# The forward transform's tail on VectorE, and the memory's denominators spread over partitions by transfers

## The chip, the core and the metric

The kernel runs on one core of a Trainium2 chip. A core has five engines that run side by side, each with its own instruction queue: TensorE (PE, with PEld for its weight loads), VectorE (DVE), ScalarE (ACT), GpSimd (POOL) and SyncE (SP), which here only issues transfers. GpSimd can issue transfers too; they go through a queue of their own (q0 in the profile, "software_dynamic"). The metric is the device time of one execution in microseconds; the times given are of several runs.

## What is computed

Two independent parts whose outputs lie side by side.

Part B multiplies a two-dimensional real spectrum by a complex filter and transforms back (x is 2048 x 576):

```
X = rfft2(x);  y = irfft2(X * (w_r + 1j*w_i), (S, D))
```

Part A is attention with 32 heads of 18 over four segments of 512, with a running memory M and its normalizer z:

```
for s in range(4):
    qs, ks, vs = q[:,:,s], k[:,:,s], v[:,:,s]
    a_dot = softmax(qs @ ks.T * scale + causal) @ vs
    pq = phi(qs);  a_mem = (pq @ M) / (pq @ z + 1e-6)
    o = g * a_mem + (1 - g) * a_dot
    M += phi(ks).T @ vs;  z += sum(phi(ks))
out = concat(o) @ wo
```

Here phi(t) is t + 1 where t > 0 and exp(t) elsewhere, and g is sigmoid(beta), one number a head.

## The kernel before

The order of instructions on every engine is the order in which the program emits them: Python generators are advanced by hand, step by step, and each step emits a few instructions. Products in full precision are made from two halves: a value is rounded to a high part (the type F32R) and the rest is its low part; high by high, high by low and low by high are then added on TensorE.

**Forward transform** (`forward`, to about 73 us). It goes over 16 units u. For each, `prep` takes the sum and the difference of two halves of the input (L125, VectorE, into eo, laid out [128, 2, 3, 128]), rounds eo to the high part h (L126/L127, ACT), and makes the low part l. The input has 289 columns: two full blocks of 128 and a third block with a tail. The low part of the two full blocks is one subtraction on VectorE (L131, 128x512). The third block carries the tail's high part and low part in different rows of the same tile: rows 64 to 96 of h are overwritten in place by their own rest, on GpSimd (L132, 33x256). `f1` then makes 14 matmuls (L142) with the tables tab and tab2, the last of each seven from the third block; `ev0` and `ev1` (L146 ACT, L149 VectorE) move the result out of PSUM, `c1` makes 12 more matmuls (L162). Between these, `load_w` splits the weights of part A: a cast on ACT (L405) and a subtraction on VectorE (L407), and for the last, half-empty block a second subtraction that makes zeros (L408). Pieces of the next stage (butterflies, L205) are taken from a paced queue. The tables are loaded on GpSimd's queue (L167 to L170), the units' input on SP's (L114).

**Projections and the inverse transform** follow (to about 356 us); the change touches them only by the second weight's last block and by the place of a small mask, bm.

**Attention** (`attention`, from about 356 us). A loop of 133 steps t. Each step emits score maxima for a later head (`s1`: matmuls L653 and L666, maxima on VectorE L667 and L661, three PSUM buffers), scores and exponentials of the current head (`s2`: L702 to L712, exponentials on ACT, and in every fourth step four causal selections on GpSimd, L716) and a product with the values (`pv`, L731). Background work is a list `bg` of generators, of which `run_bg(1.2)` advances 1.2 pieces a step. A second list, `lane`, is advanced once a step. What must come a step or two later is put off by `later`.

For the segments g = 1, 2, 3 the background is `mixed(g)`: it interleaves `combine(g-1)`, which finishes the previous segment's output, with `mem1(g,t)` for five tiles t in the order ORD = (4,0,1,2,3), then `oproj(g-1)`, the output projection (L874), in half-groups of seven matmuls. The memory's denominators come from `den` (L785), and `recip` turns them into reciprocals: load as 128x128, add 1e-6, reciprocal (L757), scale by the gate (L759), then split into three bf16 parts (L760 to L763, ACT and GpSimd), stored and loaded again as rc["rd"] with 96 rows. `mem1` then works like this:

```
nc.tensor.matmul(pn[:r],s.Mst[g][:r,t,:r],...)          # L804
(vector or scalar copy)(am[:r],pn[:r])                   # L806
yield
nc.tensor.matmul(pb[:r],s.sel[:,t,:r],s.rc["rd"],...)    # L810: sel spreads 7 heads over 126 rows
nc.vector.tensor_tensor(am[:r],am[:r],pb[:r],op=OP.mult) # L811
yield
```

pn and pb share one PSUM buffer ("post"; the score buffers from step 117 on). In `combine`, `high` (L836) and `low` (L841) split the result for the projection; the low part is on GpSimd before step 117 and on VectorE from then on, and so is the sum L857.

**The tail**, after the loop, finishes segment 3: U is copied (L737), its row sums go to memory (rD, L742) and come back, `recip` runs for them, `last_tile` (L883 to L886, L890) makes the last tiles and `last_proj` (L903) projects them, while what is left of `oproj(2)` runs.

Of the kernel before, what the change touches and what calls it, by code (L numbers as in the profile page):

```python
# [5 lines left out]
F32=mybir.dt.float32; F32R=mybir.dt.float32r  # L6
# [96 lines left out]
class FFT:  # L103
# [4 lines left out]
    def forward(s,xp,cp,pp,wl,xs,consts):  # L108
# [10 lines left out]
        def prep(u,halves=False):  # L119

            x=xin.pop(u)
            eo=xp.tile([128,2,3,128],F32,name="eo",bufs=2)
            h=xp.tile([128,2,3,128],F32R,name="eh",bufs=3)
            for r,op in enumerate((OP.add,OP.subtract)):
                v.tensor_tensor(eo[:,r],x[:,0],x[:,1],op=op)  # L125
                if halves: nc.scalar.copy(h[:,r],eo[:,r])  # L126
            if not halves: nc.scalar.copy(h,eo)  # L127
            yield
            l=xp.tile([128,2,2,128],F32R,name="el",bufs=3)
            for w in (slice(0,1),slice(1,2)) if halves else (slice(0,2),):  # L130
                v.tensor_tensor(l[:,w],eo[:,w,:2],h[:,w,:2].bitcast(F32),op=OP.subtract)  # L131
                nc.gpsimd.tensor_tensor(h[64:97,w,2],eo[64:97,w,2],h[64:97,w,2].bitcast(F32),op=OP.subtract)  # L132
            eh[u],el[u]=h,l
            yield
        def f1(u):
            p=pp.tile([128,2,512],F32,name="f1",tag="f1")
            h,l=eh.pop(u),el.pop(u)
            for r in range(2):
                L=[(h[:,r,0],tab[:,0,r,0]),(h[:,r,1],tab[:,0,r,1]),(h[:,r,0],tab[:,1,r,0]),(h[:,r,1],tab[:,1,r,1]),
                   (l[:,r,0],tab[:,0,r,0]),(l[:,r,1],tab[:,0,r,1]),(h[:99,r,2],tab2[:99,r])]  # L140
                for n,(x,t) in enumerate(L):
                    nc.tensor.matmul(p[:,r,:FP],x,t,start=n==0,stop=n==6)  # L142
            F[u]=p
# [22 lines left out]
        tab2=cp.tile([128,2,FP],F32R,name="ftab2",bufs=1)  # L166
# [173 lines left out]
        flush()  # L340
BF=mybir.dt.bfloat16
ORD=(4,0,1,2,3)
H=32; DH=18; SC=float(DH)**-0.5
NEG=-1.0e30

# [39 lines left out]
class ATT:  # L385
    def __init__(s,nc,tc,io,cp,dp):
        s.nc,s.tc,s.io=nc,tc,io
        s.ident=cp.tile([128,128],F32,name="ident"); s.bm=cp.tile([126,7,19],F32,name="bm")
        s.tri=cp.tile([128,128],BF,name="tri"); s.idb=cp.tile([128,128],BF,name="idb")
        s.Mst=[None]+[cp.tile([126,5,126],F32,name=f"Mst{i}") for i in range(1,4)]  # L390
        s.zst=[None]+[cp.tile([126,5,32],F32,name=f"zst{i}") for i in range(1,4)]
        d=lambda n,sh,dt: dp.tile(sh,dt,name=n)
        s.qkD=[d(f"qkD{i}",[8,3,128,512],BF) for i in range(4)]
        s.reD=[d(f"reD{i}",[24,32,512],BF) for i in range(4)]
        s.pqD=[None]+[d(f"pqD{i}",[576,512],F32) for i in range(1,4)]
        s.vD=[d(f"vD{i}",[4,128,622],F32) for i in range(4)]
        s.dp=dp
    def consts(s):
        nc,io=s.nc,s.io
        for i in range(1,4): nc.gpsimd.memset(s.zst[i],0.0)  # L400
        return lambda: (nc.sync.dma_start(s.ident,io["ident"]),nc.sync.dma_start(s.bm,io["bm"].rearrange("p (h c) -> p h c",h=7)))
    def wsplit(s,nm,x,t,o,w):

        nc=s.nc; h=s.wh[nm][:,t,o:o+w]; l=s.wl[nm][:,t,o:o+w]
        nc.scalar.copy(h,x)  # L405
        m=128 if t<4 else 64
        nc.vector.tensor_tensor(l[:m],x[:m],h[:m].bitcast(F32),op=OP.subtract)  # L407
        if t==4: nc.vector.tensor_tensor(l[64:],h[64:].bitcast(F32),h[64:].bitcast(F32),op=OP.subtract)  # L408
# [166 lines left out]
    def att_setup(s,cp):  # L575
        nc,io=s.nc,s.io
        s.Qs+=[cp.tile([128,8,512],BF,name=f"Qs{i}") for i in range(1,3)]
        s.Ks+=[cp.tile([128,8,512],BF,name=f"Ks{i}") for i in range(1,4)]
        s.bt,s.gt,s.g1=[cp.tile([128,1],F32,name=n) for n in ("bt","gt","g1")]
        nc.sync.dma_start(s.bt,io["beta"])  # L580
        d=lambda n,sh,dt: s.dp.tile(sh,dt,name=n)
        s.uD=[d(f"uD{i}",[576,512],F32) for i in range(4)]
        s.rD=[d(f"rD{i}",[32,512],F32) for i in range(4)]
        nc.sync.dma_start(s.rD[3][24:32],io["neg1"][0:1].rearrange("o (h c) -> (o h) c",c=512))
        s.dD=[None]+[d(f"dD{i}",[32,512],F32) for i in range(1,4)]
        s.rrD=[d(f"rrD{i}",[96,512],BF) for i in range(4)]
        s.rdD=[None]+[d(f"rdD{i}",[96,512],BF) for i in range(1,4)]

    def stacks0(s,pool):

# [147 lines left out]
    def u_dmas(s,n):  # L738
# [10 lines left out]
    def recip(s,src,dst,gate,eps,load,slack=0):  # L749
        nc=s.nc; tp=s.tp  # L750
        w=tp.tile([128,3,128],BF,name="rw",bufs=2); y=tp.tile([128,128],F32,name="ry",bufs=2)
        nc.sync.dma_start(y,src.rearrange("h (b c) -> (h b) c",b=4))
        yield
        yield
        yield
        if eps: nc.vector.tensor_scalar(y,y,1e-6,None,op0=OP.add)
# [11 lines left out]
        r=tp.tile([96,512],BF,name=load,bufs=1)  # L768
        nc.sync.dma_start(r,dst)
        s.rc[load]=r  # L770
        yield
# [6 lines left out]
    def den(s,g,lane):  # L778
# [22 lines left out]
    def mem1(s,g,t):  # L801
# [8 lines left out]
        nc.tensor.matmul(pb[:r],s.sel[:,t,:r],s.rc["rd"],start=True,stop=True)  # L810
# [15 lines left out]
    def combine(s,g):  # L826
# [5 lines left out]
        yield  # L832
        def high(u):
            r=126 if u<4 else 72
            s.oh[u]=tp.tile([128,512],F32R,name="oh",bufs=5); s.ol[u]=tp.tile([128,512],F32R,name="ol",bufs=5)
            (nc.vector.tensor_copy if s.now>=119 else nc.scalar.copy)(s.oh[u][:r],s.am[u][:r])  # L836
        def low(u):
            r=126 if u<4 else 72
            A,B=s.oh[u],s.ol[u]
            l=B if u<4 else tp.tile([128,512],F32R,name="ol4",bufs=1)  # L840
            eng().tensor_tensor(l[:r],s.am[u][:r],A[:r].bitcast(F32),op=OP.subtract)  # L841
            if u==4:
                s.later(1,lambda: nc.sync.dma_start(B[:72].bitcast(F32),A[:72].bitcast(F32)))
# [68 lines left out]
    def begin(s,sm,sp,ps1):  # L912
        s.late=[]; s.now=-1
        s.sm,s.sp,s.ps1=sm,sp,ps1
        s.mh=sm.tile([128,8,16],BF,name="mh",bufs=1); s.nc.gpsimd.memset(s.mh,0.0)
        s.mg={};s.mx={};s.m2={};s.P={};s.vs={};s.rc={};s.am={};s.pq={};s.ux={};s.potag=None
    def prologue(s):

        nc,io=s.nc,s.io
# [14 lines left out]
        assert not q  # L934
    def homes(s):

        for n,t,b in (("oh",F32R,5),("ol",F32R,5),("am",F32,5),("pq",F32,5),("ux",F32,3),("ol4",F32R,1)): s.tp.tile([128 if n in ("oh","ol","ux","ol4") else 126,512],t,name=n,bufs=b)
    def attention(s,tp,ps):
        nc=s.nc; s.tp,s.ps,s.psm,s.mtag=tp,ps,s.ps1,"s1"
        s.homes()  # L940
# [17 lines left out]
        for t in range(133):  # L958
# [7 lines left out]
            if t==34: bg.append(s.den(1,lane))  # L966
            if st==8 and g>0:
                def ln(g=g):
                    r=s.recip(s.rD[g-1],s.rrD[g-1],s.g1,False,"rr",2)
# [9 lines left out]
            if t==125: lane.append(s.recip(s.rD[3],s.rrD[3],s.g1,False,"rr"))  # L979
# [28 lines left out]
        assert not q  # L1008
        s.potag="s2"; s.last_parts()
        if qu: qu.pop(0)()  # L1010
        b=s.recip(s.rD[3],s.rrD[0],s.g1,False,"rd"); next(b)
        for u in range(3): s.ux_load(3,u)
        while qu: qu.pop(0)()
        i=0
# [138 lines left out]
```

## Time and profile before

| | us |
|---|---|
| median of 3 runs | 711.75 |
| lowest, highest | 710.95, 712.4 |
| the profiled execution | 710.93 |
| its span, first to last instruction | 709.2 |

In that execution PE was busy for 679.2 us, VectorE for 551.2, ACT for 451.3 and GpSimd for 209.8; the granted clock of TensorE was 1.00 throughout. In a profile a line such as "L131 DVE ... el<-eo,eh 128x512 ... x7 | 7.5, 1071" is one group of instructions: code line, engine, output and inputs, shape, count, busy us in total and mean ns of one, and behind the next bar the idle time in front of them. Durations of neighbouring instructions can overlap by a little, so the distance between two starts is the better measure of what one costs its engine. A busy PE is not PE at its peak.

### The profile page before, as it was taken

The page shows a single profiled execution, that of the slowest core. Times are in us where ns is not written, and L with a number is a line of the kernel's source. Part 1 is how long each engine was busy: PE and PEld are TensorE (multiplying, and loading weights), DVE is VectorE, ACT ScalarE, POOL GpSimd, SP SyncE. Part 2 cuts the span into 40 slices and gives each one's busy share as a digit, 9 for nine tenths or more (in the row PEclk, how much of TensorE's full clock was granted, in tenths as well). Part 3 has the DMA queues.
Part 4 walks back from the last instruction along what each step waited for, and adds up shares of the span by engine and source line. Part 5 has one row for each costly group of instructions (what it writes and reads, how often), then busy time and mean ns, then how long its engine had stood idle before and what let it go on. Part 6 is the DMA issues. An engine that isn't in the chain of part 4 may idle for free. (4 is left out here: it accounts for less than half of the span.)

```text
span 709.2 us, 14404 instructions
## 1 busy us (share of the span) xinstructions
PE 679.2 (96%) x4991; PEld 501.4 (71%) x4991; DVE 551.2 (78%) x1262; ACT 451.3 (64%) x986; POOL 209.8 (30%) x403
## 2 busy tenths in 40 slices
PE   4999999999999999999999899999999999999997
PEld 4988869879879879999954454445566445663487
DVE  5999979899799779787787887888657876567533
ACT  3665797485587474544378777777656776567421
POOL 5432000100200102655235333444323652235300
PEclk9999999999999999999999999999999999999999
DMA  8996455576385688899339886886656767442152
GB/s 308 289 286 171 132 159 185 162 208 203 91 234 177 167 209 294 199 253 262 110 111 207 182 175 137 197 202 159 152 131 176 190 159 158 89 127 67 28 156 82
DMA packets 71146, 123.80 MB, mean 175 GB/s; under 512 B 12184, under 2 KB 39174, under 8 KB 67482
## 3 DMA queue, kind: packets, MB, share of 16 engines
q1 hardware_dynamic: 64422, 106.89, 57.3%
q0 software_dynamic: 5632, 15.76, 8.2%
q8 instruction: 39, 0.64, 0.4%
q10 hardware_dynamic: 1020, 0.25, 0.2%
q14 instruction: 33, 0.27, 0.2%
HBM read 82.10 MB, written 39.81 MB: 172 GB/s over the span
## 5 line engine op out<-in xcount | busy, mean ns | idle before, releaser
L661 DVE CUSTOM_DVE_ANT_0 junk<-s,x 128x512 bf16<-128x512 f32 x248 | 137.0, 552 | 57.9 <-PE s L653 53.1
L716 POOL TENSOR_SCALAR_AFFINE_SELECT P<-P 128x512 f32<-128x512 f32 (+2 forms) x132 | 78.4, 625 | 113.6 <-ACT P L703 104.8
L667 DVE TENSOR_REDUCE mx<-s 128x4 f32<-128x512 f32 x128 | 87.7, 685 | 5.2 <-PE s L666 3.3
L703 ACT ACTIVATE P<-s 128x512 f32<-128x512 f32 x128 | 77.7, 607 | 12.6 <-PE s L702 4.6
L731 PE MATMUL pv<-P,vs 128*32 128x512 f32 (+3 forms) x1024 | 82.5, 439 | 0.1
L708 ACT ACTIVATE P<-s 128x512 f32<-128x512 f32 x128 | 77.5, 606 | 2.4 <-PE s L707 2.2
L712 ACT ACTIVATE P<-s 128x256 f32<-128x256 f32 x128 | 49.9, 390 | 44.7 <-PE s L711 44.2
L653 PE MATMUL s<-Ks,Qs 108*128 108x384 bf16 (+3 forms) x256 | 69.1, 301 | 1.5 <-DVE mx L667 1.2
L731 PEld LDWEIGHTS pv<-P,vs 128*32 128x32 f32 x1024 | 26.9, 109 | 45.3 <-issue 34.5
L461 PE MATMUL pj<-x,wqkh 128*128 128x512 f32 x162 | 56.5, 409 | 0.0
L653 PEld LDWEIGHTS <-Qs 108*128 108x128 bf16 x320 | 31.5, 98 | 24.4 <-issue 13.0
L205 DVE TENSOR_TENSOR Z<-t,t 128x290 f32<-128x290 f32 (+1 forms) x96 | 48.4, 555 | 0.1
L519 POOL MEMSET vt<- 128x32 f32 x16 | 2.4, 167 | 149.0 <-PE pm L529 127.7
L205 DVE TENSOR_TENSOR t<-Z 128x580 f32<-128x580 f32 x64 | 46.1, 757 | 0.0
L142 PE MATMUL f<-ftab,eh 128*128 128x290 f32 (+1 forms) x160 | 32.6, 323 | 11.8 <-DMA ftab<-ftab 9.2
L666 PE MATMUL s<-tri,idb 128*128 128x128 bf16 x256 | 43.0, 219 | 0.0
L295 PE MATMUL i<-civ,Y 128*128 128x256 f32 (+1 forms) x288 | 39.3, 289 | 0.2 <-POOL Y L280 0.2
L295 PEld LDWEIGHTS i<-civ,Y 128*128 128x128 f32 (+1 forms) x288 | 36.6, 181 | 1.0 <-POOL Y L280 0.4
L306 PE MATMUL i<-itab,T 128*128 128x290 f32 (+1 forms) x224 | 36.7, 306 | 0.0
L142 PEld LDWEIGHTS f<-ftab,eh 128*128 128x128 f32 (+1 forms) x160 | 26.1, 206 | 14.0 <-issue 8.6
L461 PE MATMUL pj<-x,wqkl 128*128 128x512 f32 x90 | 35.5, 395 | 0.0
L461 PE MATMUL pj<-xh,wqkl 128*128 128x512 f32 x90 | 35.5, 395 | 0.0
(210 smaller groups left out, 1830.2 us busy)
## 6 DMA issues: line engine op xcount, KB each, us to landing
qkD<-sp SPq DMA_DIRECT2D x32, 384.0 KB
xin<-xb SPq DMA_DIRECT2D x16, 384.0 KB
cfw<-cfw POOLq DMA_DIRECT2D x16, 384.0 KB, 4.3
civ<-civ POOLq DMA_DIRECT2D x16, 384.0 KB, 8.8
vs<-vD SPq DMA_DIRECT2D x16, 330.0 KB
vD<-vt SPq DMA_DIRECT2D x16, 311.0 KB
W<-w SPq DMA_DIRECT2D x16, 290.0 KB
yb<-yout SPq DMA_DIRECT2D x16, 290.0 KB
```

Of the source, the lines that this page charges most:

```text
L142: nc.tensor.matmul(p[:,r,:FP],x,t,start=n==0,stop=n==6)
L205: v.tensor_tensor(o,a,b,op=op)
L295: nc.tensor.matmul(p[:m,k],Y[i][:,q,c*128:c*128+m],cc[:,hl,o:o+256],start=n==0,stop=n==5)
L461: s.nc.tensor.matmul(out,a,b,start=i==0,stop=i==len(L)-1)
L653: nc.tensor.matmul(out,Q[:108,h,128*i:128*i+128],K[:108,h,:128*(i+1)],start=True,stop=True)
L661: nc.vector.tensor_tensor_reduce(out=junk[:,:w],in0=src,in1=s.mask[:,512-w:],scale=1.0,scalar=-3.0e38, op0=OP.add,op1=OP.max,accum_out=s.m ...
L667: nc.vector.tensor_reduce(out=s.mx[k][:,hh],in_=pa.rearrange("p (b c) -> p b c",c=128),axis=mybir.AxisListType.X,op=OP.max)
L703: nc.scalar.activation(P[0][:,hh],p0,AF.Exp,scale=SC)
L708: nc.scalar.activation(P[1][:,hh],p1,AF.Exp,scale=SC)
L712: nc.scalar.activation(P[2][:,hh],p2,AF.Exp,scale=SC)
L716: nc.gpsimd.affine_select(out=x[:,r],in_=x[:,r],pattern=[[0,r.stop-r.start],[1,128]],compare_op=OP.is_ge,fill=0.0,base=0,channel_multiplie ...
L731: nc.tensor.matmul(s.pvt[32*hh:32*hh+32,128*j:],vt[:,j,19*h:19*h+32],mv[0][:,hh,mv[1]],start=j==0,stop=j>1,skip_group_check=True)
```

## The change

In the forward transform h is now one of three tiles made once and set to zero in its third block by GpSimd memsets, ahead of the first loads. The high copy writes the two full blocks and, in a second instruction, rows 64 to 96 of the third; l gets the third block too, so that one subtraction on VectorE over 768 columns makes all low parts (where h is zero the difference is the value itself). `f1` takes its tail from l instead of h. GpSimd has no part in it.

The weights' last low block is set to zero by a GpSimd memset instead of a subtraction on VectorE.

In the attention part the memory's reciprocals stay f32 and go to memory as [32, 512]. `bt_load` then reads them back spread over partitions, each of 7 rows (4 in the short tile) to 18 partitions, by a transfer on GpSimd's queue into a ring bt of BT = 2 buffers. `mem1` multiplies pn in PSUM by that tile in one VectorE instruction and asks for the next load a step later. The matmul pb with sel, the copy of pn and one of its two yields go. The other reciprocals (rr, and the last rd) go through `recip` as before. To make room, rw has one buffer, bm moves to another pool, and the low part of the short tile borrows the buffer ol[3] in place of one of its own.

```diff
-            h=xp.tile([128,2,3,128],F32R,name="eh",bufs=3)
+            h=H[u%3]
+            W=(slice(0,1),slice(1,2)) if halves else (slice(0,2),)
             for r,op in enumerate((OP.add,OP.subtract)):
                 v.tensor_tensor(eo[:,r],x[:,0],x[:,1],op=op)
-                if halves: nc.scalar.copy(h[:,r],eo[:,r])
-            if not halves: nc.scalar.copy(h,eo)
-            yield
-            l=xp.tile([128,2,2,128],F32R,name="el",bufs=3)
-            for w in (slice(0,1),slice(1,2)) if halves else (slice(0,2),):
-                v.tensor_tensor(l[:,w],eo[:,w,:2],h[:,w,:2].bitcast(F32),op=OP.subtract)
-                nc.gpsimd.tensor_tensor(h[64:97,w,2],eo[64:97,w,2],h[64:97,w,2].bitcast(F32),op=OP.subtract)
+                if halves or r:
+                    w=W[r] if halves else W[0]
+                    nc.scalar.copy(h[:,w,:2],eo[:,w,:2])
+                    nc.scalar.copy(h[64:97,w,2],eo[64:97,w,2])
+            yield
+            l=xp.tile([128,2,3,128],F32R,name="el",bufs=3)
+            for w in W: v.tensor_tensor(l[:,w],eo[:,w],h[:,w].bitcast(F32),op=OP.subtract)
...
-                   (l[:,r,0],tab[:,0,r,0]),(l[:,r,1],tab[:,0,r,1]),(h[:99,r,2],tab2[:99,r])]
+                   (l[:,r,0],tab[:,0,r,0]),(l[:,r,1],tab[:,0,r,1]),(l[:99,r,2],tab2[:99,r])]
...
+        H=[xp.tile([128,2,3,128],F32R,name=f"eh{i}",bufs=1) for i in range(3)]
+        for h in H: nc.gpsimd.memset(h[:,:,2].bitcast(F32),0.0)
         load(0)
...
-        if t==4: nc.vector.tensor_tensor(l[64:],h[64:].bitcast(F32),h[64:].bitcast(F32),op=OP.subtract)
+        if t==4: nc.gpsimd.memset(l[64:].bitcast(F32),0.0)
...
+    def bt_load(s):
+        if not s.bsrc: return
+        a,t=s.bsrc.pop(0); w=7 if t<4 else 4
+        x=s.tp.tile([126,512],F32,name="bt",bufs=BT)
+        a=a[7*t]
+        s.nc.gpsimd.dma_start(x[:18*w],bass.AP(tensor=a.tensor,offset=a.offset,ap=[[512,w],[0,18],[1,512]]))
+        s.bts.append(x)
+    def recip_mem(s,g):
+        nc=s.nc; d=s.rdD[g]
+        y=s.tp.tile([128,128],F32,name="ry",bufs=2)
+        nc.sync.dma_start(y,s.dD[g].rearrange("h (b c) -> (h b) c",b=4))
+        for _ in range(3): yield
+        nc.vector.tensor_scalar(y,y,1e-6,None,op0=OP.add)
+        nc.vector.reciprocal(y,y)
+        yield
+        nc.scalar.activation(y,y,AF.Copy,scale=s.gt)
+        yield
+        nc.sync.dma_start(d.rearrange("h (b c) -> (h b) c",b=4),y)
+        for _ in range(3): yield
+        s.bsrc=[(d,t) for t in ORD]
+        for _ in range(BT):
+            s.bt_load()
+            yield
...
-            yield from s.recip(s.dD[g],s.rdD[g],s.gt,True,"rd",2)
+            yield from s.recip_mem(g)
...
-        (nc.vector.tensor_copy if s.now>=119 else nc.scalar.copy)(am[:r],pn[:r])
+        nc.vector.tensor_tensor(am[:r],pn[:r],s.bts.pop(0)[:r],op=OP.mult)
+        s.later(1,s.bt_load)
         if g<3: s.later(1,lambda: s.pq_load(g+1,t))
-        yield
-        pb=s.post("pb")
-        nc.tensor.matmul(pb[:r],s.sel[:,t,:r],s.rc["rd"],start=True,stop=True)
-        nc.vector.tensor_tensor(am[:r],am[:r],pb[:r],op=OP.mult)
...
-            l=B if u<4 else tp.tile([128,512],F32R,name="ol4",bufs=1)
+            l=B if u<4 else s.ol[3]
```

More of the change, by code (lines that the diff above doesn't have):

```diff
@@ L387, in __init__ @@
         s.nc,s.tc,s.io=nc,tc,io
-        s.ident=cp.tile([128,128],F32,name="ident"); s.bm=cp.tile([126,7,19],F32,name="bm")
+        s.ident=cp.tile([128,128],F32,name="ident")
         s.tri=cp.tile([128,128],BF,name="tri"); s.idb=cp.tile([128,128],BF,name="idb")
@@ L399, in consts @@
         nc,io=s.nc,s.io
+        s.bm=s.ftp.tile([126,7,19],F32,name="bm",bufs=1)
         for i in range(1,4): nc.gpsimd.memset(s.zst[i],0.0)
@@ L586, in att_setup @@
         s.rrD=[d(f"rrD{i}",[96,512],BF) for i in range(4)]
-        s.rdD=[None]+[d(f"rdD{i}",[96,512],BF) for i in range(1,4)]
+        s.rdD=[None]+[d(f"rdD{i}",[32,512],F32) for i in range(1,4)]
     def stacks0(s,pool):
@@ L748, in u_dmas, with recip @@
         return L
-    def recip(s,src,dst,gate,eps,load,slack=0):
+    def bt_load(s):
[21 more added lines that the diff above has]
+            yield
+    def recip(s,src,dst,gate,load,slack=0):
         nc=s.nc; tp=s.tp
-        w=tp.tile([128,3,128],BF,name="rw",bufs=2); y=tp.tile([128,128],F32,name="ry",bufs=2)
+        w=tp.tile([128,3,128],BF,name="rw",bufs=1); y=tp.tile([128,128],F32,name="ry",bufs=2)
         nc.sync.dma_start(y,src.rearrange("h (b c) -> (h b) c",b=4))
@@ L767, in recip @@
         yield
-        r=tp.tile([96,512],BF,name=load,bufs=1)
+        r=tp.tile([96,512],BF,name=load,bufs=1) if load=="rr" else tp.tile([126,512],F32,name="bt",bufs=BT)[:96].bitcast(BF)[:,:512]
         nc.sync.dma_start(r,dst)
@@ L834, in high @@
             r=126 if u<4 else 72
-            s.oh[u]=tp.tile([128,512],F32R,name="oh",bufs=5); s.ol[u]=tp.tile([128,512],F32R,name="ol",bufs=5)
+            s.oh[u]=tp.tile([128,512],F32R,name="oh",bufs=5)
+            for w in (4,3) if u==4 else (u,) if u<3 else (): s.ol[w]=tp.tile([128,512],F32R,name="ol",bufs=5)
             (nc.vector.tensor_copy if s.now>=119 else nc.scalar.copy)(s.oh[u][:r],s.am[u][:r])
@@ L935, in homes @@
     def homes(s):
-        for n,t,b in (("oh",F32R,5),("ol",F32R,5),("am",F32,5),("pq",F32,5),("ux",F32,3),("ol4",F32R,1)): s.tp.tile([128 if n in ("oh","ol","ux","ol4") else 126,512],t,name=n,bufs=b)
+        for n,t,b in (("oh",F32R,5),("ol",F32R,5),("am",F32,5),("pq",F32,5),("ux",F32,3),("bt",F32,BT)): s.tp.tile([128 if n in ("oh","ol","ux") else 126,512],t,name=n,bufs=b)
     def attention(s,tp,ps):
@@ L968, in ln @@
                 def ln(g=g):
[L969 removed]
+                    r=s.recip(s.rD[g-1],s.rrD[g-1],s.g1,"rr",2)
                     for i in range(8):
@@ L1010, in attention @@
         if qu: qu.pop(0)()
-        b=s.recip(s.rD[3],s.rrD[0],s.g1,False,"rd"); next(b)
+        b=s.recip(s.rD[3],s.rrD[0],s.g1,"rd"); next(b)
         for u in range(3): s.ux_load(3,u)
```

6 lines of the change are left out of this document (3 added, 3 removed).

## The prediction

> **What bounds the kernel now.** I began with the page: one core, the span and the engines' shares.
>
> ```profile
> span 709.2 us, 14404 instructions
> ## 1 busy us (share of the span) xinstructions
> PE 679.2 (96%) x4991; PEld 501.4 (71%) x4991; DVE 551.2 (78%) x1262; ACT 451.3 (64%) x986; POOL 209.8 (30%) x403
> ```
>
> TensorE (PE) is busy for 96% of the span, so the question for each edit is whether, in its own stage, PE is waiting for what the edit takes away. The change touches three stages: the forward transform (up to about 73 us), the attention loop where memory tiles are combined (three times), and the tail. So I read busy time by stretches, first the forward's.
>
> ```profile
> 30.00:35.00 5.00, 5.00 (x39) 5.00 (x38) 4.71 (x9) 2.65 (x5) 1.93 (x3) 1.00 0.83 270
> 45.00:50.00 5.00, 4.70 (x35) 4.46 (x34) 5.00 (x8) 3.29 (x6) 2.11 (x4) 1.00 0.78 247
> 65.00:70.00 5.00, 5.00 (x37) 5.00 (x38) 4.34 (x8) 3.00 (x6) 0.53 (x1) 1.00 0.75 202
> ```
>
> The columns are PE, PEld, DVE (VectorE), ACT, POOL (GpSimd), clock, DMA share, GB/s. At 30 us PE is full; at 45 us VectorE is full and PE has gaps; at 65 us PE is full again. Between lies a stretch bound by VectorE. How long a unit takes there is seen from the starts of the f1 matmuls.
>
> ```profile
> 32.50 0.70 PE L142 MATMUL f<-ftab,eh 128*128 128x290 f32 x4
> ...
> 36.02 0.70 PE L142 MATMUL f<-ftab,eh 128*128 128x290 f32 x4
> ...
> 64.97 0.80 PE L142 MATMUL f<-ftab,eh 128*128 128x290 f32 x4
> ```
>
> A unit at PE's pace takes 36.02 − 32.50 = 3.52 us. The next seven took 64.97 − 36.02 = 28.95 us where PE alone needs 24.64. So up to 4.3 us can be had by making VectorE faster, and no more.
>
> **Part 1, the forward's tail.** The groups of VectorE in the stretch 35 to 64 us, and one instruction's smallest, median and largest duration over the whole run:
>
> ```profile
> L131 DVE TENSOR_TENSOR el<-eo,eh 128x512 fp32r<-128x512 f32 x7 | 7.5, 1071 | 0.0
> L125 DVE TENSOR_TENSOR eo<-xin 128x384 f32<-128x384 f32 x13 | 6.6, 547 | 0.0
> L407 DVE TENSOR_TENSOR wqkl<-raw,wqkh 128x576 fp32r<-128x576 f32 (+1 forms) x7 | 6.3, 903 | 0.0
> ...
> L408 DVE TENSOR_TENSOR wqkl<-wqkh 64x576 fp32r<-64x576 f32 x2 | 1.5, 756 | 0.0
> ```
> ```profile
> L131 DVE TENSOR_TENSOR el<-eo,eh x18: 414/692/1230, 6.1 to 61.4; 128x512 fp32r<-128x512 f32 x14, 128x256 fp32r<-128x256 f32 x4
> L407 DVE TENSOR_TENSOR wqkl<-raw,wqkh x10: 741/1016/1300, 25.2 to 62.0; 128x576 fp32r<-128x576 f32 x8, 64x576 fp32r<-64x576 f32 x2
> ```
>
> L131 takes 0.69 us at its median and up to 1.23; L407 takes 0.74 or 1.30. The extra 0.55 us falls on whichever of them meets GpSimd's subtraction of the tail (L132): the two engines' two-input instructions take turns. Removing L132 gives back 7 x (1.071 − 0.692) + 7 x (0.903 − 0.741) = 2.65 + 1.13 = 3.8 us in this stretch. The low subtraction grows from 512 to 768 elements; L125 against L131 gives (0.692 − 0.547)/128 = 1.13 ns an element, so 0.29 us each, 2.0 us in seven. Replacing L408 by a GpSimd memset takes 1.5 us off VectorE. Sum: −3.8 + 2.0 − 1.5 = −3.3 us, below the 4.3 that PE can give. I take −3.2; bounds −4.3 and −1.5 (L408 alone). The high copy on ACT becomes two instructions; ACT is busy for 3.29 of 5 us there, which hides it; if it did not, VectorE would wait for it, about 0.1 us a unit.
>
> The same exchange for the second weight near 90 us saves two further subtractions; PE is almost full there. I take −0.3, between −0.9 and 0.
>
> Against this stands the start. Three memsets of 128x256 now go ahead of the table loads in GpSimd's queue, and PE's first matmuls wait for those tables:
>
> ```profile
> L400 POOL MEMSET zst<- x3: 258/258/259, 2.0 to 2.4; 126x160 f32 x3
> ```
> ```profile
> PE f L142 <- DMA ftab<-ftab: 9.2, 2, 8.3
> ```
>
> Three memsets of 160 columns take 0.26 us each and start some 0.2 us apart, so three of 256 delay the loads by about 0.8 us (1.24 at most). The DMA engines meanwhile go on with the xin loads, so part of it comes back: I take +0.6, between 0 and 1.2.
>
> **Part 2, the memory's denominators in the attention loop.** Now the stretches of the first and second combination (463 to 500, 556 to 592), of output projection (500 to 545) and of a loop with no background work (547 to 556), and the exponentials (one of L703 a step) in the first:
>
> ```profile
> 463.00:500.00 37.00, 35.41 (x291) 17.57 (x284) 29.41 (x86) 27.23 (x64) 17.31 (x29) 1.00 0.78 179
> 500.00:545.00 45.00, 45.00 (x382) 29.68 (x380) 27.93 (x81) 28.11 (x68) 13.29 (x28) 1.00 0.59 142
> 547.00:556.00 9.00, 9.00 (x90) 4.49 (x89) 7.71 (x24) 6.81 (x17) 3.72 (x6) 1.00 0.88 201
> 556.00:592.00 36.00, 34.43 (x270) 17.38 (x266) 28.32 (x82) 26.03 (x61) 20.18 (x30) 1.00 0.78 181
> ```
> ```profile
> 463.00:500.00 37.00, 8.53 (x14) 1.00 0.78 179
> ```
>
> PE holds the pace in all of them, with 1.6 us of gaps in each combination. What goes: 15 matmuls pb (L810), the copy of pn in front of each product, and three split operations of GpSimd per reciprocal. What stays is one VectorE product a tile, now of pn in PSUM and the spread reciprocal in SBUF. What a pb costs PE is the distance to the next matmul:
>
> ```profile
> 655.55 0.38 PE L810 MATMUL pb<-rd,sel 96*126 96x512 bf16 x1
> 655.77 0.27 PE L711 MATMUL s<-x,Ks 110*128 110x256 bf16 x1
> ```
>
> That is 0.22 us: ten pb in the first two combinations are −2.2 us; with a little of the gaps that stood around them I take −2.4 (bounds: −1 if VectorE, busy for 29.4 of 37 us, is the next limit; −4 if most gaps go too). Walking the generators, one combination has 14 background pieces instead of 19, so the rest of the background comes about four steps earlier in the loop; that moves work and removes none.
>
> What is added: 15 transfers of 126x512 f32 (252 KB) on GpSimd's queue into a ring of two buffers. The first two of each group are loaded well ahead; the other nine are issued when a buffer comes free. A wait for one stands in front of VectorE's product, and behind it on VectorE are the maxima of the next score tiles, so PE runs out of score buffers (three) about a step later.
>
> The room: a tile is used every 2 pieces, at 1.2 pieces a step of 37/14 = 2.6 us, so every 4.4 us; from a product to the use of the same buffer two tiles on 8.8 us. But the issue is emitted a step later, behind what GpSimd then has:
>
> ```profile
> L716 POOL TENSOR_SCALAR_AFFINE_SELECT P<-P 128x512 f32<-128x512 f32 x16 | 9.7, 633 | 7.6 <-ACT P L703 7.0 <-PE s L653 0.5
> L841 POOL TENSOR_TENSOR ol<-am,oh 126x512 fp32r<-126x512 f32 (+1 forms) x5 | 6.4, 1272 | 9.8 <-ACT oh L836 9.8
> ```
>
> four selections in every fourth step (2.5 us) and a low part (1.27 us) that waits for ACT. That leaves some 3 to 6 us, on average 4. What landing takes, from issues on the same queue (KB each, median us to landing):
>
> ```profile
> cfw<-cfw POOLq DMA_DIRECT2D x16, 384.0 KB, 4.3
> civ<-civ POOLq DMA_DIRECT2D x16, 384.0 KB, 8.8
> ...
> sel<-sel POOLq DMA_DIRECT2D x1, 118.1 KB, 3.0
> ...
> Ks<-neg POOLq DMA_DIRECT2D x3, 16.0 KB, 10.3
> ```
>
> Between 3.0 and 10.3 us. Nearest in size and DMA load is cfw; with the odd shape (7 rows, each to 18 partitions) I take 5.0, so 1 us late on average, 9 us for nine. PE's buffers ahead absorb more than half of that: +3.5, bounds 0 and +12.
>
> [...]
>
> **Part 3, the third combination and the tail.** Here steps no longer compute scores, and the four earlier steps bring five half-groups of the output projection in front of the last pv instead of after it. So the loop ends later by their time and the tail has that much less to do; as long as PE stays busy the two cancel, and the five pb that go here too remain, 5 x 0.22 = 1.1 us. The tail's own chain decides whether PE stays busy:
>
> ```profile
> 671.45 0.69 DVE L737 COPY U<-pv 128x512 f32<-128x512 f32 x1 [1.76 <-PE pv L731]
> 681.21 0.69 DVE L884 TENSOR_TENSOR ux<-ux,pb 126x512 f32<-126x512 f32 x1 [9.06 <-DMA ux<-uD]
> ```
> ```profile
> 673.45 0.33 SPq L769 DMA_DIRECT2D rr<-rrD x1
> 673.87 0.56 SPq L742 DMA_DIRECT2D rD<-U x1
> ```
> ```profile
> 687.73 0.29 PE L903 MATMUL po<-woh,P 126*128 126x288 f32 x1
> ```
>
> From the copy of U to the first product are 9.8 us, to the first last_proj matmul 16.3 us, filled with projection. With less filling PE would wait for that chain; but SP sends rD 1.7 us after the copy has finished, held behind the reciprocal's rr, which with fewer instructions ahead of it on VectorE should be gone by then. I take −1.0, the five pb; bounds −2.5 (most of those 1.7 us as well) and +1.5 (PE standing still for the part of the moved work that the chain does not allow for).
>
> **The sum.** Against the profiled execution: 710.93 us, span 709.2 and 1.7 us around it. +0.6 − 3.2 − 0.3 − 2.4 + 3.5 − 1.0 = −2.8, so 708.1. The median of the runs is 711.75, 0.8 above; I forecast 708.9 us.
>
> **The rivals.** First: the transfers land in time. Then the +3.5 falls away: 705.4. For it: cfw's median, 4.3 us, is near the room of 4, and DMA is less busy in the third combination. Against: the bulk of GpSimd's instructions in front of them. [...]
>
> Second, on the other side: few DMA engines carry a transfer and it lands in about 7 to 8 us, between cfw's 4.3 and civ's 8.8 and towards the latter. Then each of nine is 3 to 4 us late, and beyond about 1.5 us each late microsecond passes to PE: 9 x 1.7 = 15 us. It decides where a landing exceeds about 6 us. The sum is then −6.3 + 15 = +8.7, so 720 at worst; where waiting lengthens the steps, and with them the room, about half: 714.
>
> Third: the forward gives nothing, since the longer low part, the two ACT copies and the later tables use up what L132 frees: −3.2 becomes −0.5, which makes 711.6, about where it was.
>
> **How the numbers follow.** Forecast 0.45, in time 0.27, late transfers 0.18, no gain in the forward 0.10. About 0.2% (1.4 us) is what a measurement of this kernel can tell from no change. Of the forecast's share 0.38 lies below 710.3 and 0.05 about the old time, a little above it; the first rival is all faster, the second nearly all slower, the third mostly the same: faster 0.65, same 0.12, slower 0.23. The range 703.5 to 714.5 holds the forecast, the first rival and the milder half of the second.
>
> **What would show it.** Right: L132 gone, L131 near 0.98 us with no long ones, f1 starts in the forward about 3.8 us apart instead of 4.1, the forward's end some 2.6 us earlier, no L810. VectorE's waits should name the new transfer with a few us in total in front of the product of am; their length decides between the forecast (about 9 us), the first rival (under 2) and the second (over 20). Wrong would be an unchanged pace of f1 starts, a first matmul over 1.2 us later, or a tail in which PE stands still for several us before the first L903.

## The result and the profile after

The changed kernel took 721.15 us (median of 5 runs, 718.34 to 721.97) against 710.95 us before (five runs of it, taken beside these): a ratio of 1.0133, 95% interval 1.0116 to 1.015. It is slower by 10.2 us where 708.9 was forecast, and lies outside the range. The profiled execution took 718.34 us. In what follows, times are medians; they and the ratios both leave the few disturbed runs out, but are formed differently and can differ by a few tenths of a per cent.

The page of the changed kernel: span, then busy time by engine.

```profile
span 716.6 us, 14382 instructions
PE 681.9 (95%) x4976; PEld 503.0 (70%) x4976; DVE 542.7 (76%) x1254; ACT 450.4 (63%) x990; POOL 200.4 (28%) x398
```

VectorE has 8.5 us less to do and PE has 15 matmuls fewer, and yet PE is busy for longer: its matmuls must have been slower somewhere.

The forward did what was forecast. The same three stretches (columns PE, PEld, DVE, ACT, POOL, clock, DMA share, GB/s), the starts of f1, and VectorE's groups between 35 and 64 us:

```profile
30.00:35.00 5.00, 5.00 (x39) 5.00 (x38) 4.50 (x8) 3.88 (x8) 1.06 (x2) 1.00 0.91 277
45.00:50.00 5.00, 4.94 (x37) 4.70 (x36) 5.00 (x9) 3.97 (x8) 0.53 (x1) 1.00 0.97 305
65.00:70.00 5.00, 5.00 (x39) 5.00 (x38) 4.04 (x7) 3.51 (x7) 0.00 (x0) 1.00 0.86 248
```
```profile
33.18 0.70 PE L143 MATMUL f<-ftab,eh 128*128 128x290 f32 x4
...
36.69 0.70 PE L143 MATMUL f<-ftab,eh 128*128 128x290 f32 x4
...
62.88 0.69 PE L143 MATMUL f<-ftab,eh 128*128 128x290 f32 x4
```
```profile
L133 DVE TENSOR_TENSOR el<-eo,eh 128x768 fp32r<-128x768 f32 x7 | 6.7, 953 | 0.1
L412 DVE TENSOR_TENSOR wqkl<-raw,wqkh 128x576 fp32r<-128x576 f32 (+1 forms) x7 | 5.2, 750 | 0.0
```

Seven units now take 62.88 − 36.69 = 26.19 us where they took 28.95, a gain of 2.8, and the two subtractions no longer have long instances (L412's mean is 750 ns, not 903). The stretch begins 0.7 us later and ends 2.1 us earlier.

The loss is in the attention loop, and most plainly in the combinations. The four stretches of the attention loop, shifted to where their work now lies:

```profile
461.00:498.00 37.00, 32.76 (x234) 15.91 (x227) 24.81 (x70) 20.50 (x48) 16.61 (x26) 0.91 0.89 185
498.00:543.00 45.00, 44.88 (x383) 29.32 (x385) 27.52 (x82) 27.89 (x67) 11.16 (x23) 1.00 0.56 128
545.00:554.00 9.00, 9.00 (x85) 4.84 (x83) 8.03 (x24) 7.33 (x18) 3.93 (x8) 1.00 0.98 227
556.00:592.00 36.00, 31.68 (x232) 15.27 (x234) 25.92 (x72) 21.91 (x50) 21.62 (x31) 0.95 0.82 186
```

In the first combination PE is idle for 4.2 us instead of 1.6, DMA share is 0.89 instead of 0.78, and the granted clock is 0.91: the same 37 us hold 234 of PE's records instead of 291. In the second, PE is idle for 4.3 us instead of 1.6. Twice in the first combination and once in the second the trace's clock records have 0.50 for 3.413 us. Cutting finer, into stretches of that length, shows that a stand (PE standing idle, waiting) was paid for twice here. First the stretch at 463 us and the one behind it, then two more at half clock, then the two that lie just ahead of these:

```profile
463.29:466.70 3.41, 1.59 (x13) 0.77 (x11) 2.62 (x8) 1.65 (x6) 0.68 (x3) 1.00 0.97 166
466.70:470.10 3.40, 3.40 (x23) 1.23 (x22) 1.19 (x4) 1.32 (x3) 1.26 (x1) 0.50 0.93 184
...
490.60:494.00 3.40, 3.40 (x10) 1.42 (x8) 1.16 (x6) 0.60 (x1) 0.77 (x3) 0.50 0.85 181
582.75:586.15 3.40, 3.40 (x16) 1.19 (x19) 2.20 (x8) 1.41 (x4) 0.60 (x3) 0.50 0.92 179
```
```profile
487.18:490.59 3.41, 1.56 (x12) 0.79 (x10) 2.17 (x6) 2.82 (x7) 1.86 (x3) 1.00 1.04 198
579.33:582.74 3.41, 1.31 (x11) 0.69 (x9) 1.75 (x5) 2.50 (x6) 3.02 (x5) 1.00 1.04 211
```

Where PE was busy for 1.3 to 1.6 of 3.41 us, the next 3.41 us ran at half the clock; each such stretch is, as an estimate, worth up to 3.41 x 0.50 = 1.7 us on top of the stand that set it off. Each time the DMA share was 0.97 to 1.04 (it adds up packets' times, so it can pass 1). The waits over the new transfers, and PE's longest ones between 440 and 690 us (engine, line, released by: total us, times, longest):

```profile
DMA to landing us min/median/max: 3.7/6.0/11.5
```
```profile
POOL bt L760 <- DVE am L835: 9.7, 5, 4.0
DVE am L835 <- DMA bt<-rdD: 5.7, 2, 3.2
```
```profile
PE s L658 <- DVE mg L666: 3.2, 2, 1.9
PE s L658 <- DMA ux<-uD: 2.8, 2, 1.8
```

VectorE waited 5.7 us for late transfers. The longer of these waits ended just ahead of the third stretch at half clock, and PE stood behind it, as the prediction had described:

```profile
580.99 0.69 DVE L835 TENSOR_TENSOR am<-pn,bt 126x512 f32<-126x512 f32 x1 [3.18 <-DMA bt<-rdD]
```
```profile
582.08 0.27 PE L658 MATMUL s<-x 108*128 108x256 bf16 x1 [1.89 <-DVE mg L666]
```

But PE's score matmul L658 was also held by a transfer itself. It reads only Qs and Ks, so the row with ux names a neighbour. The trace's record of landings settles which load it was. Of the four loads that fill its Qs, the last was issued as follows, before the change and after it:

```profile
459.79 0.39 SPq L637 DMA_DIRECT2D Qs<-reD  x1
```
```profile
456.75 0.39 SPq L642 DMA_DIRECT2D Qs<-reD  x1
```

Before, it landed at 466.14 us, 6.4 us after the issue; now at 465.44 us, 8.7 us after it, and the matmul that had been waiting since 463.87 us started at 465.69 us. That the prediction had not priced.

### The profile page after: what moved, and what is told of

Its sections match the earlier page's. It is cut to its first block, busy times and chain, and to the rows that moved or that the text cites. A ratio compares the mean times of both kernels' runs of the same rounds, so it can differ in the third digit from the quotient of the medians.

```text
span 716.6 us, 14382 instructions
## 1 busy us (share of the span) xinstructions
PE 681.9 (95%) x4976; PEld 503.0 (70%) x4976; DVE 542.7 (76%) x1254; ACT 450.4 (63%) x990; POOL 200.4 (28%) x398
## 3 DMA queue, kind: packets, MB, share of 16 engines
q0 software_dynamic: 8032, 19.31, 10.2%
## 5 line engine op out<-in xcount | busy, mean ns | idle before, releaser
L736 PE MATMUL pv<-P,vs 128*32 128x512 f32 (+3 forms) x1024 | 84.3, 447 | 0.1
L658 PE MATMUL s<-Ks,Qs 108*128 108x384 bf16 (+3 forms) x256 | 69.7, 303 | 1.7 <-DMA ux<-uD 1.0
L658 PEld LDWEIGHTS <-Qs 108*128 108x128 bf16 x320 | 31.5, 99 | 24.8 <-issue 11.6
L658 PE MATMUL s<-Ks,x 108*128 108x384 bf16 (+3 forms) x128 | 35.1, 303 | 0.7 <-DMA x<-reD 0.6
L466 PE MATMUL pj<-xh,wqkh 128*128 128x512 f32 x90 | 35.5, 395 | 0.0
```

Source lines behind the costliest of these rows:

```text
L466: s.nc.tensor.matmul(out,a,b,start=i==0,stop=i==len(L)-1)
L658: nc.tensor.matmul(out,Q[:108,h,128*i:128*i+128],K[:108,h,:128*(i+1)],start=True,stop=True)
L736: nc.tensor.matmul(s.pvt[32*hh:32*hh+32,128*j:],vt[:,j,19*h:19*h+32],mv[0][:,hh,mv[1]],start=j==0,stop=j>1,skip_group_check=True)
```

## Experiments

Each kernel is timed beside the kernel before, whose median was then 710.6 to 711.0 us. A difference between two rows is good to 2 to 3 us.

| kernel | median us | ratio to before (95%) |
|---|---|---|
| forward's part alone | 709.54 | 0.9979 (0.9959 to 0.9999) |
| attention's part alone | 726.11 | 1.0208 (1.0167 to 1.0249) |
| no late loads | 713.64 | 1.0042 (1.002 to 1.0064) |
| six copies, 42 outer rows | 720.98 | 1.014 (1.0101 to 1.0178) |
| no late loads, early pair | 713.33 | 1.0033 (1.001 to 1.0056) |
| shared ring of seven | 723.29 | 1.0153 (1.0114 to 1.0192) |
| ring and early pair | 721.18 | 1.0138 (1.0105 to 1.017) |
| 19 pieces | 712.03 | 1.0015 (0.9989 to 1.004) |
| no transfers, 14 pieces | 707.70 | 0.9961 (0.994 to 0.9983) |
| no transfers, 19 pieces | 704.17 | 0.9915 (0.9889 to 0.994) |
| half the bytes, 14 pieces | 712.77 | 1.0047 (1.0013 to 1.0081) |
| forward, memsets on VectorE | 708.63 | 0.9976 (0.9949 to 1.0002) |
| nobody waits, 14 pieces | 715.76 | 1.0064 (1.0041 to 1.0087) |
| nobody waits, 19 pieces | 713.54 | 1.0027 (1.0001 to 1.0052) |
| half the bytes, 19 pieces, two buffers | 706.03 | 0.9933 (0.9914 to 0.9952) |
| the same, four buffers | 707.77 | 0.9953 (0.9934 to 0.9971) |

**The two parts apart.** The forward's functions of one kernel were put into the other, with the weight's split.

> The kernel before with the forward's part of the change alone (low part by one VectorE subtraction, high copy in two instructions, three memsets ahead of the table loads, the weight's low half by a GpSimd memset); the attention loop is as before. Theory 1 (the loss is all in the attention loop): the 2.1 us that the changed kernel had gained at its first exponential stay to the end, and 0.3 of the second weight is among them: 708.5 to 709.0 us against 710.95, ratio 0.997. Theory 2 (an earlier attention loop meets its transfers less ready, so the gain is lost later): 710.5 to 711.5.

> The changed kernel with the forward and the weight's split of before; the attention's part of the change alone. Theory 1: the time of the changed kernel plus the 2.1 us that the forward gave, 723 us, ratio 1.017. Theory 2 (the two parts make each other worse): below 720.

The forward alone is 1.4 us faster, the attention's part alone 15 us slower; together 10.2. The loss is all in the attention's part, so the first theory held, with a gain somewhat smaller than put down. A forward that ends earlier did not make the loop worse; without it the attention's part cost even more than the 723 put down. So the two parts do not simply add (15.2 − 1.4 = 13.8, not 10.2); why is not shown.

**The start.** `nc.gpsimd.memset(h...)` became `v.memset(h...)` in the forward-only kernel.

> The forward's part alone, with the three memsets on VectorE, which is idle until the first input lands at 4.0 us, instead of ahead of the table loads on GpSimd's queue. Theory (the memsets delay the table loads and PE's start by 1.2 to 1.4 us, of which about half is lost for good): the first f1 matmul near 8.3 us instead of 9.5, time 708.5 to 709.2 against 709.5. Rival (the start is set by the loads' own competition): no change in the first matmul, 709.5.

The first f1 matmul, forward alone and then with the memsets on VectorE:

```profile
9.51 0.82 PE L143 MATMUL f<-ftab,eh 128*128 128x290 f32 x2 [9.51 <-DMA ftab<-ftab]
```
```profile
8.95 0.82 PE L143 MATMUL f<-ftab,eh 128*128 128x290 f32 x2 [8.95 <-DMA ftab<-ftab]
```

It came 0.56 us earlier, not 1.2: about half of the delay is the memsets' place; the other 0.6 us against 8.33 is not explained. The ratios to before, 0.9976 and 0.9979, can't be told apart.

**Are the late transfers the loss?** Three of five transfers of each group were left out:

```
-  s.bsrc=[(d,t) for t in ORD]
+  s.bsrc=[(d,t) for t in ORD[:BT]]; s.bts=[]
...
-  ... s.bts.pop(0)[:r],op=OP.mult)
-  s.later(1,s.bt_load)
+  ... s.bts[ORD.index(t)%BT][:r],op=OP.mult)
```

> The changed kernel with only the first two of the five transfers of each group; the last three products of a group multiply by one of these two tiles again, so nine of fifteen transfers (2.3 MB) are left out, and three fifths of the memory part is scaled by another head's reciprocals. Theory 1 (the loss is the wait for transfers that are late, with the clock that falls in PE's gaps): 711 minus 2.1 of the forward, minus 1.2 in each of the first two cycles, plus 0.6 in the third and the tail: 707, and VectorE's waits for the spread reciprocals are under 2 us in total. Rival (14 background pieces in place of 19 pack each combination so that VectorE, SP's queue and PE's score buffers are late anyway): 716 or more, with the same falls of the clock.

713.64, between the two. The largest wait of PE in the loop, in a kernel in which no product is seen waiting for a transfer:

```profile
PE s L658 <- DMA Qs<-reD: 3.1, 1, 3.1
```

Late loads of Qs, then, even with only the pair loaded ahead. I supposed that this pair was badly placed, and moved it (`if t==22` for `if t==34` at the first group's denominators).

> The kernel without the nine late transfers (three fifths of the memory part scaled by another head's reciprocals), and the first group's denominators started at step 22 instead of 34, so that the pair of transfers loaded ahead goes at about 434 us, where the DMA share was 0.2, instead of 457 us, where it is 0.9 to 1.1 and the score block's own loads (Qs, Ks) are on their way. Theory A (what was left, 713.8 against the 709.5 of the forward alone, is this pair delaying Qs<-reD, for which PE stood 3.1 us, and the clock that fell after it): the exponentials gain 3 to 4 us between steps 51 and 55: 709.5 to 711. Rival (the packing of the combination into fewer steps): no gain there, 713 to 714.5.

713.33: no gain that can be told. The stand did not vanish, it moved: with the pair issued at 432 to 434 us, the DMA share is 1.03 to 1.12 between 435 and 445 us, and PE stands 1.54 us at a score matmul at 450.5 us, with half the clock behind it. The rival's time came out; what the trace shows is the same collision further ahead, and not the packing.

**Few engines?** Six copies of each row in DRAM (393 KB written for each group instead of 64, well ahead of the loads), `ap=[[512,6*w],[0,3],[1,512]]` for `[[512,w],[0,18],[1,512]]`.

> The changed kernel with six copies of each reciprocal row in DRAM (written by four transfers instead of one, 393 KB instead of 64 KB a group, long ahead), so that a spread load has 42 outer rows read three times each instead of 7 read 18 times; bytes and queue of the load are the same. [...] Theory 1 (few engines carry the load): median landing falls from 6.0 us to 4 to 4.5, and with it half of the waits: 713 to 715 us. Rival (the DMA engines as a whole are full, 0.89 to 0.98 busy there, and GpSimd issues late): landing stays at 5.5 to 6.5, time 719 to 722.

Landing times in the quiet third group (649 to 675 us), changed kernel and then six copies, and over all groups with six copies:

```profile
DMA to landing us min/median/max: 3.7/3.8/4.0
```
```profile
DMA to landing us min/median/max: 3.1/3.3/3.6
```
```profile
DMA to landing us min/median/max: 3.1/5.4/9.7
```

Where DMA is quiet, the packets of one transfer ran for 2.05 us with 5.6 in flight on average before this edit and 1.45 us with 9.5 to 10.1 after it, and the landing fell from 3.8 to 3.3 us. So the edit did put more packets in flight at a time and shortened the transfer. Over all groups the median landing fell by 0.6 us and the kernel's time not at all, so the second rival had the right sign and nearly the right size for a wrong reason.

**More room.** Products are made in the buffer that the transfer filled; loads follow each low part (`s.fr.append(s.am[u]); s.bt_load()`), from a ring of seven.

> The changed kernel with one ring of seven buffers for the spread reciprocals and the combined tiles (two and five before, the same memory): a transfer lands in the buffer in which the product is then made, and the third to fifth of a group are issued when the low part of an earlier tile has been made on GpSimd, some two pieces (about 4 us) earlier than when a product frees one of two. All fifteen transfers and all results as in the changed kernel. Theory A (the room of about 4 us is too short for landings of 6 to 11 us): VectorE's and GpSimd's waits over the spread reciprocals, 15 us in sum, fall under 4, and the time to 714 to 717, with the loss at steps 51 to 55 left. Rival (transfers issued earlier collide with the loads of Qs and Ks just as well): 719 or more.

> The shared ring of seven buffers and the first group's denominators from step 22 together, all else as in the changed kernel. Theory A (two causes that add: the late transfers and the first pair): 709 to 712, no stretch of 5 us in the first combination with a granted clock under 0.9. Rival (packing, or the bytes themselves): 715 or more.

VectorE's longest wait at the product, with the ring:

```profile
DVE am L835 <- PE pn L833: 11.6, 10, 2.5
```

No row there names the transfer any more: the products' own wait is gone, and yet the kernel took 723.29 us. Theory A fell. With the early pair, 721.18 us, again the rival's time; PE's longest waits between 440 and 690 us are again at the score matmul, and again on DMA:

```profile
PE s L658 <- DMA uD<-U: 3.9, 1, 3.9
PE s L658 <- DMA Ks<-qkD: 2.2, 1, 2.2
PE s L658 <- DMA x<-reD: 1.8, 1, 1.8
```

**Packing and bytes.** A second `yield` behind `s.am[t]=am` makes 19 pieces again. Without transfers, `s.bsrc=[]` and the product multiplies by `s.one`, a tile of ones.

> The changed kernel with the second yield of each product put back, so that a combination has 19 background pieces again as before and products stand one piece (about 2.2 us) further apart; transfers and buffers as in the changed kernel. Theory A (room): five steps more between a release and its use, waits over the reciprocals fall by about half, 716 to 719, and the loss at steps 51 to 55 stays. Rival (the packing into 14 pieces was the loss): 709 to 712, the offset of the exponentials at step 55 no more than 1 us above that at step 50.

> The changed kernel without any of the fifteen spread loads: each product of the memory part multiplies by a tile of ones, so the memory part stays undivided; 14 pieces a combination as in the changed kernel. Theory B (the 3.6 MB added to DMA engines that were 0.8 to 1.0 busy delay the score block's own loads, PE stands and its clock falls; the packing is harmless by itself): 706 to 708, no stretch with a clock under 0.9 in the first two combinations. Rival (14 pieces bring VectorE's and SP's work too close together even without the transfers): 711 to 714, as with six of fifteen transfers left (713.3 and 713.8).

> As the kernel without spread loads, but with 19 pieces a combination again. Theory B: within 1.5 us of the one with 14 pieces, 706 to 708.5. Rival (packing): 706 to 708 too, but then 4 us or more below the one with 14 pieces.

> The changed kernel with the reciprocals stored, spread and multiplied as bf16 (rounded, so the memory part is less exact): fifteen transfers of the same 126 rows, of 1 KB instead of 2 KB each, 14 pieces, two buffers. Theory B (bytes): about half of the distance between the changed kernel, 721.2, and the one without transfers: 713 to 716. Rival (the number of transfers and of their rows, or GpSimd's issues, and not the bytes): 719 to 722.

By its time the rival of the 19 pieces came out (712.03), and theory B of the kernel without transfers (707.70). Without transfers, 19 pieces gained 3.5 us more, between what theory (at most 1.5) and rival (4 or more) had put down. So both count, and they aggravate each other: the transfers cost 13.5 us with 14 pieces (721.15 − 707.70) and 7.9 with 19 (712.03 − 704.17); the packing costs 3.5 us without transfers and 9.1 with them. Half the bytes in the same number of transfers and rows leave 5.1 of the 13.5 us, so it is mostly the bytes. The two combinations without transfers, 14 pieces:

```profile
455.00:492.00 37.00, 36.12 (x289) 18.61 (x286) 30.75 (x88) 26.07 (x62) 16.62 (x28) 1.00 0.79 193
550.00:586.00 36.00, 34.98 (x275) 18.94 (x273) 27.76 (x79) 24.26 (x57) 21.79 (x30) 1.00 0.74 172
```

PE's gaps are back to about 1 us and the clock is full. The load Qs<-reD, issued at 456.58 us here, landed in 6.5 us, against 8.7 with the transfers. Part of what packing costs by itself is seen in the tail. Every trace of 14 pieces has 3.4 to 6.8 us at half clock some 23 to 25 us before its end, behind a stand of PE; none of 19 pieces has, nor has the kernel before. Without transfers, 14 pieces:

```profile
678.17:681.58 3.41, 1.02 (x4) 0.51 (x3) 3.34 (x6) 2.32 (x7) 0.43 (x1) 1.00 0.03 11
681.58:684.99 3.41, 3.11 (x13) 3.11 (x14) 2.98 (x5) 0.93 (x2) 1.72 (x3) 0.50 0.56 169
```

The starts of the first exponential of a step against the kernel before, less the offset at step 0 (−2.1, −0.7 and −1.4 us), place the loss of the loop (profiled executions, us):

| step | 52 | 60 | 84 | 116 | 127 |
|---|---|---|---|---|---|
| changed kernel | 0.4 | 3.1 | 5.8 | 9.0 | 9.0 |
| no late loads | −0.6 | 3.4 | 2.8 | 3.2 | 3.2 |
| no transfers, 14 pieces | 0.0 | −0.5 | −1.2 | −3.1 | −3.1 |

**Whose wait?** All transfers are issued as in the changed kernel, but the product multiplies by a column of ones: `s.bts.pop(0)` and `s.one[:r].to_broadcast([r,512])`.

> The changed kernel with all fifteen transfers issued at the same places into the same two buffers, but each product multiplies by a column of ones (the memory part stays undivided), so no product waits for a transfer. Theory C (the price is the products' own wait for late transfers): 709 to 712, near the 707.7 without transfers. Theory D (the price is in the loads of Qs, Ks and ux, delayed by the added bytes): 716 to 721, with PE's waits at the score matmuls and the falls of the clock as in the changed kernel.

> The changed kernel with 19 pieces, all fifteen transfers issued, and each product multiplying by a column of ones (the memory part stays undivided). Theory C (the products' own waits): 704 to 706, as without transfers. Theory D (delayed loads of Qs, Ks and ux): 709 to 712, as with transfers, with PE waiting at the score matmuls for these loads.

With 14 pieces 715.76, with 19 pieces 713.54. Against the kernels without transfers that is 8.1 and 9.4 us (by the ratios 7.3 and 8.0) for transfers that nobody waits for. They lie 3.8 and 7.5 us above theory C's ranges and within 2 us of theory D's, so theory D holds in kind. The products' own wait, with GpSimd's wait for the buffer that follows from it, adds 5.4 us with 14 pieces (721.15 − 715.76) and nothing that can be told with 19. One part of theory D did not show in the 19-piece trace: the late load (ux, on SP's queue) held ACT, and PE waited behind ACT instead of for the load itself:

```profile
ACT P L708 <- DMA ux<-uD: 4.5, 1, 4.5
PE s L707 <- ACT P L708: 3.5, 4, 2.7
```

In the 19-piece kernel without transfers ACT has no such wait.

Stretches of 50 us, 19 pieces, nobody waits:

```profile
450.00:500.00 50.00, 46.80 (x373) 22.95 (x372) 38.51 (x112) 32.97 (x78) 22.24 (x40) 0.93 0.86 189
...
550.00:600.00 50.00, 46.42 (x390) 23.95 (x389) 38.77 (x111) 33.07 (x80) 29.33 (x45) 1.00 0.89 194
```

and without transfers:

```profile
450.00:500.00 50.00, 48.16 (x411) 24.20 (x411) 43.04 (x126) 36.76 (x88) 22.12 (x41) 1.00 0.78 185
...
550.00:600.00 50.00, 47.82 (x401) 25.25 (x400) 38.20 (x110) 33.14 (x79) 26.45 (x40) 1.00 0.71 167
```

A DMA share of 0.86 and 0.89 instead of 0.78 and 0.71, and PE is busy for 1.4 us less in each; where the clock falls too, it does less in that time as well.

**A version that gains.** Reciprocals in bf16, 19 pieces, memsets on VectorE; then four buffers of half the size.

> The changed kernel with bf16 reciprocals (rounded, so the memory part is less exact), 19 pieces a combination, and the forward's three memsets on VectorE. From the runs: 19 pieces without transfers 704.2, with all bytes 712.0, half of the distance 708.1, less 0.7 for the memsets: 707.4, ratio 0.995. If the bytes count less than in proportion: 705 to 706. If the two don't add: 710 or more.

> The same with four buffers of 1 KB a row in the memory of the two of 2 KB. Theory (room matters besides bytes): fewer waits for the spread reciprocals than with two buffers and 0.5 to 1.5 us less time, 706 to 707. Rival (four transfers ahead crowd the start of a combination): the same as with two buffers or above.

706.03 us is the best of all with the whole computation in it, 5 us below the kernel before, though with rounded reciprocals. Four buffers gave no gain over two, as the rival had it: room was not what was missing.

## Why the prediction was wrong

- **Start, forward and weight, forecast −2.9:** right in mechanism. The stretch behind VectorE gained 2.8 us where 3.2 was taken. The forward alone measured −1.4 by its median, and the changed kernel's first exponential came 2.1 us earlier (354.45 us instead of 356.58 us in the traces). L412 came out as the 0.75 us that was forecast, L133 at 0.953 instead of 0.98, the f1 starts 3.74 us apart on average where 3.8 was named. The first matmul was 1.4 us later (9.72 instead of 8.33 us), more than the bound of 1.2, of which half was made up by 33 us.
- **Fifteen pb and the moved work, forecast −3.4:** measured −1.8 (707.70 without transfers, less 709.54 of the forward alone). Without transfers the exponentials gained 1.2 us up to step 84 and 1.9 more up to step 116, the 2.4 forecast and a little more. But "moves work and removes none" was too easy: 14 pieces cost 3.5 us against 19, with no transfer in play.
- **The transfers, forecast +3.5, bounds 0 and +12:** 13.5. This is the step that failed. The price of the products' own wait was of the right order (5.4 us, the clock behind it included). What was left out is the other side: the prediction quoted DMA shares of 0.78 in both combinations and 0.88 in the loop between them and asked only when the new transfer would land, not what lands later because of it. That is 8.1 us: with a share of 0.89 in the first combination the load Qs<-reD landed in 8.7 us instead of 6.4, and PE's next scores waited for it; in the 19-piece trace a late ux held ACT. The clock that halved behind a stand (0.50 for 3.413 us, three times in the two combinations) was not in the sum either. How the 8.1 us divide between the stands and the clock is not measured.
- **Third combination and tail, forecast −1.0:** about +0.6 in the profiled execution (exponentials 6.8 us late at step 116, which is the 9.0 of the table less 2.1; the span 7.4 us longer). PE did stand just before the first last_proj at 691.78 us, for 1.8 us where the prediction had named several as a mark of being wrong, and what followed ran at half clock. DMA was quiet here; PE waited for the tail's own chain (L911 on VectorE), as it did without any transfers:

```profile
691.75 0.40 PE L910 MATMUL pb<-rr,sel 96*126 96x512 bf16 x1 [1.76 <-DVE ux L911]
```

```profile
688.57:691.98 3.41, 1.40 (x9) 0.97 (x9) 3.03 (x5) 1.52 (x5) 0.00 (x0) 1.00 0.15 58
```
```profile
691.98:698.80 6.82, 6.37 (x27) 6.02 (x26) 3.77 (x6) 1.73 (x4) 2.15 (x3) 0.50 0.58 165
```

- **Rivals.** The first (in time, 705.4) was excluded by landings of 6.0 us; even with no transfers at all the changed kernel's packing stood at 707.7. The second came nearest in time (714, at worst 720); its cause, few engines, was tested and is not it. (Half of its 15 us would give 713 by its own sum, not 714.) Its landing of 7 to 8 us was an estimate; the changed kernel showed 6.0 us at the median and 3.8 where DMA was quiet. No run shows the 1.5 us that it let each transfer be late at no cost to PE. The third is out for the forward's stretch, which gained 2.8 us; in the kernel's time half of the forecast −2.9 came through. VectorE's waits for the transfer, 5.7 us, lay between what the forecast (9) and the first rival (under 2) had named, and decided nothing: the wait to look at was PE's.

The shares −1.4, −1.8 and +13.5 add up to the measured +10.2 by construction, since each is the difference of two neighbouring kernels, so their sum confirms nothing; another order gives other shares (the attention's part alone costs 15.2). What stays open: why the two parts do not add, how packing and transfers aggravate each other, and half of the later start.

## What to carry to other kernels

Before a transfer is put in place of work on an engine, price it twice: when it lands, and what it makes late. Here the DMA share of the stretch was near 0.8 and PE's operands came by DMA in that very stretch, and the added bytes were paid by these operands. To tell the two prices apart, issue the transfer and let nobody wait for it. And packing the same work into fewer steps isn't free: it cost 3.5 us here with no transfer in play.

## What the hardware showed that was not expected

A short stand cost more than itself here. Two rows of PE in the changed kernel's timeline (start, us; the wait in brackets), and one of the kernel before:

```profile
465.69 0.32 PE L658 MATMUL s<-x,Qs 108*128 108x384 bf16 x1 [1.82 <-DMA ux<-uD]
...
466.78 2.36 PE L736 MATMUL pv<-P,vs 128*32 128x512 f32 x16
```
```profile
458.42 1.28 PE L731 MATMUL pv<-P,vs 128*32 128x512 f32 x16
```

PE stood for 1.82 us at one go; after a stretch of 3.41 us with 1.59 us of work the next one went at clock 0.50, and sixteen pv matmuls took 2.36 us instead of 1.28. Three stretches in the two combinations and 6.8 us in the tail went so; in the trace's clock records each of the three lasts 3.413 us and the one in the tail 6.827. They begin at 466.70, 490.59, 582.75 and 691.98 us, which lie 7, 27 and 32 times 3.413 us apart. Of this kernel's stretches counted in this way, the least busy one in the loop behind which the clock stayed full was this, with 62%:

```profile
555.44:558.85 3.41, 2.10 (x21) 1.03 (x13) 3.00 (x11) 2.21 (x6) 2.25 (x5) 1.00 1.01 190
```

The stretches ahead of the four falls were not idle: PE was busy for 38 to 47% of each (1.31 to 1.59 of 3.41 us). Why the clock fell behind these and not behind the one with 62%, this trace does not show.
